# Last three third-matrix groups as split products, with the next attention and some remainders moved

## The chip, the cores and the metric

The kernel runs on one core of a Trainium2 chip. The metric is the device time of one execution in microseconds. Three runs of the kernel before took 1400.58 to 1402.51 us, median 1401.87 us. A separate profiled execution took 1403.44 us; the span of the kernel's own instructions in it is 1401.6 us.

## The reference

Attention without softmax, then two feed-forward stages, all in float32. Eight batches of eight heads, 576 tokens, 64 values per head:

```
kv  = einsum('bhsd,bhse->bhde', k, v)
out = einsum('bhsd,bhde->bhse', q, kv)
out = out / sqrt(mean(out*out, -1) + 1e-6) * g_norm
x   = out as (4608 tokens, 512)
g   = softplus(x @ w_in)                     # 512 -> 2048
x   = g @ w_out                              # 2048 -> 512
h   = max(x @ w1, x @ w2, x @ w3)            # 512 -> 768, three matrices
y   = h @ moe2_w_out                         # 768 -> 512
```

The weights arrive as float64 words and are made into float32 on the chip.

## The kernel before, in words

The tokens are done in five passes (`run_pass`), each of two halves of 456 or 464 tokens. A pass runs four layers in turn: the first (H groups, `w_in`), the second (X groups, `w_out`), the third (nine groups 16 to 24, three matrices for each of three row blocks, ended by an elementwise maximum) and the output layer. Every 2x2 block product is done in seven products instead of eight (numbered 1 to 7), so right sides and weights need sums and differences first (`combine`, `combine32`, `sums_of_weights`).

A product comes in two forms. In the first pass it is float32: two matmul calls of one column block each, which the profile shows as two instructions each, so four per product; the left side is the float32 sum of weights `sw`. In the later passes it is split: each operand is a float32r part `hi` and a float32r remainder `lo`, and a product has three float32r matmuls per block (`mm3`, lines 137 to 139), six in all. The split weights are kept as units: `make_unit` (line 302) casts a pair of sums on ScalarE (line 121) and subtracts on GpSimd (line 127), and `keep_first` stores the unit to memory for the later passes. For groups from `LATE` on, the sums themselves are stored (`keep_sums`) and the second pass splits them (`split_ahead`, `keep_ahead`).

The weights of the first pass go through these steps: SP loads raw words (line 239); ScalarE makes two parts of them (lines 250 and 252); VectorE joins them into `sw` (lines 257 and 261); GpSimd makes the four other sums (lines 130 and 133); then products read them and units are made. There are three buffers of `sw`, three of raw words, four of units `u` and two of single units `u3`.

The attention of the next pass runs beside the third layer of this one (`attention_beside`, line 654): kv products of a batch (line 471), `kv_evict` with two casts and two subtractions, and for each of eight pairs of a half and a head pair a q load, `split_q`, six matmuls `out_mm`, `square`, two matmuls `ssq_mm` and `norm`.

The order is written out by hand. Each step is put down with `at(t, ...)`, where t counts slots of one product each; the nine groups of the third layer begin at `base2`, seven slots apart, and `base2` is slot 119 of the first pass. Steps are issued in the order of t. A scheduler then orders each engine's instructions by readiness, except where an engine is pinned to the written order: all engines up to slot 1, SP for most of the kernel, and SP and ScalarE from two slots before the third layer of the first pass to its end. Slots are an order and no times: an engine goes on when its inputs are there.

Of the kernel before, what the change touches and what calls it, by code (L numbers as in the profile page):

```python
# [8 lines left out]
F32 = mybir.dt.float32  # L9
F32R = mybir.dt.float32r  # L10
# [25 lines left out]
SLOT = {1: 0, 5: 1, 6: 3, 2: 4, 7: 6, 4: 9, 3: 12}  # L36
ORDER = (1, 5, 6, 2, 7, 4, 3)
U_BUFS, U3_BUFS, GE_BUFS = 4, 2, 14
LATE = 23
FIRST_SLOT = {1: -72.2, 2: -71.5, 5: -71, 6: -69.3, 7: -67, 4: -66.4, 3: -66}  # L40
FIRST_DONE = {2: -67.9}
SECOND_SLOT = {**SLOT, 1: -75, 2: -73.7}
# [7 lines left out]
def kernel(  # L50
# [181 lines left out]
        return [w123[2 * f + i, j] for i in range(2)]  # L232

    raws, jobs = {}, []
    BESIDE = {(2, 0), *((g, 1) for g in range(1, 15) if g != 2)}

    def load_raw(key, src):
        raw = pools["raw"].tile([P, DM, 2], I32, tag="raw", bufs=3, name="raw")
# [53 lines left out]
    def sums_of_weights(g, halves=(0, 1)):  # L292
        w = sw[g]
        a11, s1, s2, a12, s3, a22, s4 = (w[:, place(g)[m]] for m in (1, 5, 6, 2, 7, 4, 3))
        if 0 in halves:
            sub(nc.gpsimd, s3, a11, s1)
            add(nc.gpsimd, s1, s1, a22)
        if 1 in halves:
            sub(nc.gpsimd, s2, s1, a11)
            sub(nc.gpsimd, s4, a12, s2)  # L300

    def make_unit(g, k):
        ms = UNITS[k]
        u = unit_tile(len(ms), 0)
        j = PLACE[ms[0]]
        src = sw[g][:, j:j + len(ms)]
        hi, lo = u[:, :, 0:256], u[:, :, 256:512]
        split(nc.scalar, src, hi, lo, nc.gpsimd)
        units[0, (g, k)] = u

    def keep_first(key):
# [52 lines left out]
    def product(p, g, m, rhs, banks):  # L364
        tag = BANK[m]
        first = m in (1, 5, 2)
        if first:
            banks[tag] = psum(tag, f"{tag}{'hxo'[(g >= 8) + (g >= 16)]}")
        acc = banks[tag][:, 0:NS[p]]
        if p == 0:  # L370
            w = sw[g][:, PLACE[m]]
            for c in range(2):
                nc.tensor.matmul(acc, w[:, c * P:(c + 1) * P], rhs[m, c], start=first and c == 0,  # L373
                                 stop=c == 1, skip_group_check=not first)
            return
        k, i = UNIT_OF[m]
        u = units[p, (g, k)]
        for c in range(2):
            xh, xl = rhs[m, c]
            wh, wl = u[:, i, c * P:(c + 1) * P], u[:, i, 256 + c * P:256 + (c + 1) * P]  # L380
            mm3(acc, wh, wl, xh, xl, first and c == 0, c == 1, not first)
# [272 lines left out]
    def attention_beside(pas, t0):  # L654

        n = NS[pas]

        for t, tt, dts in ((0, t0 - 9, (0, 2, 6, 9)), (1, t0 + 16, (0, 3, 6, 9))):
            for b in new_batches(pas, t):

                for p in range(NP):
                    at(tt + (dts[p] - 10 if p < 2 else dts[p - 2] + 0.15), load_kv, b, p)
                    at(tt + dts[p] + 0.1, kv_mm, b, p)
                at(tt + dts[3] + (0.2 if t == 0 else 1.35), kv_evict, b)
        for k in range(2 * NP):
            h, p = divmod(k, NP)
            a = TOK[pas] + h * n
            t = t0 + 8 + 6 * k
            at(t - (12 if pas == 1 else 6), load_q, a, n, p)
            at(t - 3, split_q, a, n, p)  # L670
            at(t + 0.3, out_mm, a, n, p)
            at(t + 0.4, square, a, n, p)
            at(t + 4.8, ssq_mm, a, n, p)
            at(t + 4.9, norm, a, n, p)

    def run_pass(pas, base):
# [5 lines left out]
        def weights_at(t, g, slot=SLOT):  # L682
            if pas == 0:
                for i in range(2 if g > 2 else 0):
                    jobs.append((t - 9 + 3 * i, (g, i), raw_of(g)[i], convert, (g, i)))
                if g > 2:
                    at(t - 5.9, sums_of_weights, g)
                if g >= LATE:
                    at(t + 1, keep_sums, g)
                for k in range(4 if g < LATE else 0):  # L690
                    tk = t + 1.6 * k + (4 if g > 15 else 0)
                    at(tk if g else (-69.1, -57, -56.5, -56)[k], make_unit, g, k)
                    at(tk + (2.5 if g > 15 else 5) if g else (3, 9, 9.5, 10)[k], keep_first, (g, k))
            else:
                for k, ms in enumerate(UNITS):

                    own = k == 0 and g != 17
                    lead = (8 if g == 0 else 5.9) if own else LEAD
                    at(t + min(slot[m] for m in ms) - lead, load_unit, pas, (g, k), len(ms), own)
# [89 lines left out]
        def combine_max(fp, steps):  # L789
# [5 lines left out]
            else:  # L795
                tile = ctile if steps in ((0,), (2,)) else partial(ge_tile, pas)
                combine(tile, R3, fp, tiles, steps, None, (1, 2, 7, 4, 3))

        for k in range(9):
            fp, j = divmod(k, 3)  # L800
            t = base2 + 7 * k
            slot = {**SLOT, 3: 9.9} if k == 8 else SLOT
            if pas and k < 2:
                slot = {**SLOT, 1: -6, 2: -1.8} if k == 0 else {**SLOT, 1: -10}
            weights_at(t, G_2[fp][j], slot)
            run_group(t, pas, G_2[fp][j], R2,
                      sums(lambda w, src, fp=fp, j=j: h2_done(fp, j, w, src),
                           lambda w, j=j: ((ge_tile(pas, f"m{w}", N), True) if j == 0
                                          else (ctile(f"m{w}", N), w == 22))), slot)
# [137 lines left out]
    at(T[7] + 0.75, sums_of_weights, 0, (0,))  # L947
    at(T[7] + 0.8, first_x, 1, 5)
    at(T[8] + 0.85, first_x, 0, 6)
    at(T[8] + 0.855, sums_of_weights, 0, (1,))  # L950
    at(T[8] + 0.86, first_x, 0, 7)
    at(T[9] + 0.25, first_x, 1, 6)
    at(T[9] + 0.86, first_x, 1, 7)
# [39 lines left out]
    for t, _, fn, args in events:  # L993
# [2 lines left out]
            pools["ge"] = ctx.enter_context(tc.tile_pool(name="gep", bufs=1, reuse_waits="tile"))  # L996
        if t < PIN:
            pinned(fn, args)
        elif third - 2 <= t < bases[1] - 1:
            pinned(fn, args, (mybir.EngineType.SP, mybir.EngineType.Activation))  # L1000
        elif t < GATE or fn in (kv_mm, load_kv) and t < bases[1]:
            with after([i for e, i in last.items() if e is not mybir.EngineType.SP]):
# [69 lines left out]
```

## Time and profile before

| what | us |
|---|---|
| median of three runs | 1401.87 |
| the profiled execution | 1403.44 |
| its span | 1401.6 |
| TensorE busy | 1382.8 |
| VectorE busy | 815.9 |
| ScalarE busy | 747.4 |
| GpSimd busy | 722.5 |

PE is TensorE, DVE is VectorE, ACT is ScalarE, POOL is GpSimd, SP issues most DMAs. The profile is of one execution; times in it count from the start of the span. The first pass takes about the first 350 us, its third layer about 213 to 326 us. A name such as Xo<-t,sw says what an instruction writes and reads: X, Y and W are the result banks, and the letter behind is h, x, o or y for the four layers. In the rows, "[0.57 <-DVE og L571]" is idle time of the engine just before the instruction, and what ended it.

### The profile page before, as it was taken

How to read it: one execution, taken by the hardware profiler on the slowest of the kernel's cores; microseconds unless marked ns; L12 is line 12 of the kernel's file. 1: busy time of each engine (PE TensorE's matmuls, PEld its weight loads, DVE VectorE, ACT ScalarE, POOL GpSimd, SP SyncE). 2: the span in 40 equal slices, each digit the busy share in tenths (PEclk: the TensorE clock that was granted, in tenths of full speed). 3: DMA queues.
4: the chain of work that ended last, by engine and by line, in shares of the span. 5: the costliest groups of instructions: out<-in, count | busy, mean ns of one | idle time of the engine just before them, and what ended most of it. 6: DMA issues, size and time to landing. Idle time of an engine off the chain costs nothing.

```text
span 1401.6 us, 18519 instructions
## 1 busy us (share of the span) xinstructions
PE 1382.8 (99%) x6086; PEld 1108.9 (79%) x6086; DVE 815.9 (58%) x1291; ACT 747.4 (53%) x1427; POOL 722.5 (52%) x658
## 2 busy tenths in 40 slices
PE   8999999999999999999999999999999999999998
PEld 6444455554788889888888898888888888999897
DVE  5655566886455656754457477455556764457544
ACT  6776626784465446636443565464446645443332
POOL 3899776777364444444345343353464434335320
PEclk9999999999999999999999999999999999999999
DMA  7588687886799867576667875866676667666675
GB/s 279 203 299 285 249 299 280 291 277 196 263 331 332 306 230 263 193 261 217 205 211 227 264 236 165 283 208 207 209 233 207 196 229 237 213 211 209 210 210 179
DMA packets 122143, 336.51 MB, mean 240 GB/s; under 512 B 13120, under 2 KB 33472, under 8 KB 122048
## 3 DMA queue, kind: packets, MB, share of 16 engines
q1 hardware_dynamic: 121472, 334.35, 72.2%
q8 instruction: 49, 0.80, 0.2%
q10 hardware_dynamic: 576, 0.98, 0.2%
q14 instruction: 46, 0.38, 0.1%
HBM read 269.88 MB, written 65.40 MB: 239 GB/s over the span
## 4 chain that ended last, share of the span: by engine, by line
PE 89%; DMA 4%; POOL 3%; DVE 2%; ACT 1%; issue 1%; SPq 0%; POOLq 0%; DVEq 0%
PE Xo L137 4%; PE Xo L373 4%; PE Xo L138 4%; PE Xo L139 4%; PE Xx L137 4%; PE Xx L139 4%; PE Xx L138 4%; PE Xh L137 4%; PE Xh L138 4%; PE Xh L139 4%; PE Xx L373 3%; PE Xh L373 2%; PE Yo L373 2%; PE Yo L139 2%; PE Yo L138 2%; PE Yo L137 2%
## 5 line engine op out<-in xcount | busy, mean ns | idle before, releaser
L127 POOL TENSOR_TENSOR lo<-e,hi 128x464 fp32r<-128x464 f32 (+1 forms) x160 | 188.1, 1208 | 183.9 <-ACT hi L121 172.4
L121 ACT COPY m<-Xo 128x464 f32<-128x464 f32 (+1 forms) x135 | 72.8, 545 | 107.2 <-PE Xo L139 75.0
L121 ACT CAST hi<-t 128x464 fp32r<-128x464 f32 (+1 forms) x120 | 65.7, 548 | 116.9 <-DVE e L133 48.0
L127 POOL TENSOR_TENSOR u<-sw,u 128x512 fp32r<-128x512 f32 x92 | 109.9, 1216 | 20.0 <-ACT u L121 20.0
L130 DVE TENSOR_TENSOR x<-x,Xx 128x464 f32<-128x464 f32 (+1 forms) x120 | 75.5, 632 | 57.7 <-PE Xx L139 52.2
L133 POOL TENSOR_TENSOR e<-e 128x464 f32<-128x464 f32 (+1 forms) x40 | 47.4, 1186 | 104.2 <-DVE t L133 103.7
L127 DVE TENSOR_TENSOR lo<-t,hi 128x464 fp32r<-128x464 f32 (+1 forms) x120 | 76.0, 637 | 35.2 <-ACT hi L121 33.1
L121 ACT CAST hi<-e 128x464 fp32r<-128x464 f32 (+1 forms) x160 | 85.5, 583 | 20.1 <-PE Yx L138 16.8
L137 PE MATMUL Xo<-hi,u 128*128 128x464 f32 (+1 forms) x224 | 84.6, 380 | 1.1 <-ACT m L121 0.6
L130 DVE TENSOR_TENSOR Wh<-h,Wh 128x464 f32<-128x464 f32 (+1 forms) x40 | 25.7, 642 | 98.9 <-PE Wh L139 72.9
L138 PE MATMUL Xo<-lo,u 128*128 128x464 f32 (+1 forms) x224 | 83.1, 371 | 0.0
L139 PE MATMUL Xo<-hi,u 128*128 128x464 f32 (+1 forms) x224 | 83.0, 371 | 0.0
L157 ACT ACTIVATE e<-h 128x464 f32<-128x464 f32 (+1 forms) x80 | 47.3, 592 | 65.5 <-DVE h L130 65.0
L133 POOL TENSOR_TENSOR sw<-sw 128x256 f32<-128x256 f32 x84 | 67.3, 801 | 20.7 <-DVE sw L261 11.0
L127 POOL TENSOR_TENSOR lo<-m,hi 128x464 fp32r<-128x464 f32 (+1 forms) x40 | 47.8, 1213 | 58.3 <-ACT hi L121 58.3
L121 ACT COPY h<-Xh 128x464 f32<-128x464 f32 (+1 forms) x108 | 58.5, 544 | 31.7 <-PE Xh L139 28.3
L614 POOL TENSOR_TENSOR og<-og,r 128x464 f32<-128x464 f32 (+1 forms) x32 | 41.5, 1298 | 62.0 <-DVE r L610 62.0
L138 PE MATMUL Xh<-lo,u 128*128 128x464 f32 (+1 forms) x194 | 72.5, 374 | 0.0
L137 PE MATMUL Xh<-hi,u 128*128 128x464 f32 (+1 forms) x194 | 72.2, 372 | 0.0
L139 PE MATMUL Xh<-hi,u 128*128 128x464 f32 (+1 forms) x194 | 72.0, 371 | 0.0
L137 PE MATMUL Xx<-hi,u 128*128 128x464 f32 (+1 forms) x192 | 71.4, 372 | 0.0
L139 PE MATMUL Xx<-hi,u 128*128 128x464 f32 (+1 forms) x192 | 71.3, 371 | 0.0
(269 smaller groups left out, 4122.3 us busy)
## 6 DMA issues: line engine op xcount, KB each, us to landing
u<-wd SPq DMA_DIRECT2D x241, 512.0 KB, 4.5
ux<-wd SPq DMA_DIRECT2D x99, 512.0 KB, 3.6
wd<-u SPq DMA_DIRECT2D x69, 512.0 KB, 5.4
u<-wd SPq DMA_DIRECT2D x104, 256.0 KB, 4.0
raw<-in_w_out_dram SPq DMA_DIRECT2D x22, 512.0 KB, 4.5
k<-in_kp_dram SPq DMA_DIRECT2D x31, 320.0 KB, 5.2
v<-in_vp_dram SPq DMA_DIRECT2D x29, 320.0 KB, 5.7
raw<-in_w_dram SPq DMA_DIRECT2D x18, 512.0 KB, 4.6
```

Of the source, the lines that this page charges most:

```text
L121: nc.scalar.copy(hi, src)
L127: eng_lo.tensor_tensor(out=lo, in0=src, in1=hi.bitcast(F32), op=ALU.subtract)
L130: eng.tensor_tensor(out=o, in0=a, in1=b, op=ALU.add)
L133: eng.tensor_tensor(out=o, in0=a, in1=b, op=ALU.subtract)
L137: nc.tensor.matmul(acc, wh, xh, start=first, stop=False, skip_group_check=on)
L138: nc.tensor.matmul(acc, wh, xl, start=False, stop=False, skip_group_check=on)
L139: nc.tensor.matmul(acc, wl, xh, start=False, stop=last, skip_group_check=on)
L157: tables["used"].append(nc.scalar.activation(out, src, func, **kw).ins)
L373: nc.tensor.matmul(acc, w[:, c * P:(c + 1) * P], rhs[m, c], start=first and c == 0, stop=c == 1, skip_group_check=not first)
L614: nc.gpsimd.tensor_tensor(out=og, in0=og, in1=r, op=ALU.mult)
```

## The change

It has these parts:

1. `FAST = 22`: in the first pass, groups 22, 23 and 24 (the last matrix row block of the third layer) take split products of six float32r matmuls instead of float32 ones. Their right sides are split by the new `split_third`: 14 casts on ScalarE, and 14 remainders in turn on VectorE and GpSimd; eight of them stand early in the third layer, six shortly before their use.
2. `LATE` goes from 23 to 25: groups 23 and 24 get units in the first pass, stored like the others, and the second pass splits only the output layer's weights ahead. `FAST_LEAD` places the units of groups 22 to 24 some 3.2 to 4 slots before their product; those of group 21 lose their delay of four slots.
3. The attention of the second pass is moved: the first pair 22 slots sooner, with seven slots from pair to pair instead of six; the kv products of its two halves 15 and 18.5 slots sooner. ScalarE and SP are pinned to the written order from 28 slots before the third layer instead of two.
4. In all later passes the first q load of a pass stands four slots earlier.
5. The third unit (products 7 and 4) of groups 2 to 11 has its remainder on VectorE instead of GpSimd.
6. One conversion (14, 1) uses another result bank.
7. At the start, the sums of group 0 are made in another order on GpSimd: one of them before the difference of the state that stood ahead of it.

```diff
@@ -36,7 +36,8 @@
 SLOT = {1: 0, 5: 1, 6: 3, 2: 4, 7: 6, 4: 9, 3: 12}
 ORDER = (1, 5, 6, 2, 7, 4, 3)
 U_BUFS, U3_BUFS, GE_BUFS = 4, 2, 14
-LATE = 23
+LATE = 25
+FAST, FAST_LEAD = 22, (3.4, 3.2, 3.2, 4)
 FIRST_SLOT = {1: -72.2, 2: -71.5, 5: -71, 6: -69.3, 7: -67, 4: -66.4, 3: -66}
 FIRST_DONE = {2: -67.9}
 SECOND_SLOT = {**SLOT, 1: -75, 2: -73.7}
@@ -232,7 +233,7 @@
         return [w123[2 * f + i, j] for i in range(2)]
 
     raws, jobs = {}, []
-    BESIDE = {(2, 0), *((g, 1) for g in range(1, 15) if g != 2)}
+    BESIDE = {(2, 0), *((g, 1) for g in range(1, 14) if g != 2)}
 
     def load_raw(key, src):
         raw = pools["raw"].tile([P, DM, 2], I32, tag="raw", bufs=3, name="raw")
@@ -295,8 +296,9 @@
         if 0 in halves:
             sub(nc.gpsimd, s3, a11, s1)
             add(nc.gpsimd, s1, s1, a22)
-        if 1 in halves:
+        if 1 in halves or 2 in halves:
             sub(nc.gpsimd, s2, s1, a11)
+        if 1 in halves or 3 in halves:
             sub(nc.gpsimd, s4, a12, s2)
 
     def make_unit(g, k):
@@ -305,7 +307,7 @@
         j = PLACE[ms[0]]
         src = sw[g][:, j:j + len(ms)]
         hi, lo = u[:, :, 0:256], u[:, :, 256:512]
-        split(nc.scalar, src, hi, lo, nc.gpsimd)
+        split(nc.scalar, src, hi, lo, nc.vector if k == 2 and 1 < g < 12 else nc.gpsimd)
         units[0, (g, k)] = u
 
     def keep_first(key):
@@ -367,7 +369,7 @@
         if first:
             banks[tag] = psum(tag, f"{tag}{'hxo'[(g >= 8) + (g >= 16)]}")
         acc = banks[tag][:, 0:NS[p]]
-        if p == 0:
+        if p == 0 and g < FAST:
             w = sw[g][:, PLACE[m]]
             for c in range(2):
                 nc.tensor.matmul(acc, w[:, c * P:(c + 1) * P], rhs[m, c], start=first and c == 0,
@@ -655,7 +657,8 @@
 
         n = NS[pas]
 
-        for t, tt, dts in ((0, t0 - 9, (0, 2, 6, 9)), (1, t0 + 16, (0, 3, 6, 9))):
+        early = pas == 1
+        for t, tt, dts in ((0, t0 - (24 if early else 9), (0, 2, 6, 9)), (1, t0 + (-2.5 if early else 16), (0, 3, 6, 9))):
             for b in new_batches(pas, t):
 
                 for p in range(NP):
@@ -665,8 +668,8 @@
         for k in range(2 * NP):
             h, p = divmod(k, NP)
             a = TOK[pas] + h * n
-            t = t0 + 8 + 6 * k
-            at(t - (12 if pas == 1 else 6), load_q, a, n, p)
+            t = t0 + (-14 + 7 * k if early else 8 + 6 * k)
+            at(t - (12 if pas == 1 else 6 if k else 10), load_q, a, n, p)
             at(t - 3, split_q, a, n, p)
             at(t + 0.3, out_mm, a, n, p)
             at(t + 0.4, square, a, n, p)
@@ -688,7 +691,9 @@
                 if g >= LATE:
                     at(t + 1, keep_sums, g)
                 for k in range(4 if g < LATE else 0):
-                    tk = t + 1.6 * k + (4 if g > 15 else 0)
+                    tk = t + 1.6 * k + (4 if 15 < g < FAST - 1 else 0)
+                    if g >= FAST:
+                        tk = t + slot[UNITS[k][0]] - FAST_LEAD[k]
                     at(tk if g else (-69.1, -57, -56.5, -56)[k], make_unit, g, k)
                     at(tk + (2.5 if g > 15 else 5) if g else (3, 9, 9.5, 10)[k], keep_first, (g, k))
             else:
@@ -796,6 +801,24 @@
                 tile = ctile if steps in ((0,), (2,)) else partial(ge_tile, pas)
                 combine(tile, R3, fp, tiles, steps, None, (1, 2, 7, 4, 3))
 
+        fast = {}
+
+        def split_third(m, c, i):
+            n = NS[0]
+            hi = xc_tile("hi", n, F32R)
+            if i < 4:
+                lo = ap_.tile([P, NC, P], F32, tag="kv", bufs=4, name="lo").rearrange("p c d -> p (c d)")
+                lo = lo[:, 0:n].bitcast(F32R)
+            else:
+                lo = (gc_tile if i < 8 else xc_tile)("lo", n, F32R)
+            split(nc.scalar, R2[m, c], hi, lo, nc.gpsimd if i % 2 else nc.vector)
+            fast[m, c] = (hi, lo)
+
+        if pas == 0:
+            for i in range(14):
+                m, c = divmod(i, 2)
+                m = ORDER[m]
+                at(base2 + (9 + 2.6 * i if i < 8 else 7 * 6 + SLOT[m] - 7 + 3.2 + c), split_third, m, c, i)
         for k in range(9):
             fp, j = divmod(k, 3)
             t = base2 + 7 * k
@@ -803,7 +826,7 @@
             if pas and k < 2:
                 slot = {**SLOT, 1: -6, 2: -1.8} if k == 0 else {**SLOT, 1: -10}
             weights_at(t, G_2[fp][j], slot)
-            run_group(t, pas, G_2[fp][j], R2,
+            run_group(t, pas, G_2[fp][j], fast if pas == 0 and G_2[fp][j] >= FAST else R2,
                       sums(lambda w, src, fp=fp, j=j: h2_done(fp, j, w, src),
                            lambda w, j=j: ((ge_tile(pas, f"m{w}", N), True) if j == 0
                                           else (ctile(f"m{w}", N), w == 22))), slot)
@@ -947,7 +970,8 @@
     at(T[7] + 0.75, sums_of_weights, 0, (0,))
     at(T[7] + 0.8, first_x, 1, 5)
     at(T[8] + 0.85, first_x, 0, 6)
-    at(T[8] + 0.855, sums_of_weights, 0, (1,))
+    at(T[8] + 0.845, sums_of_weights, 0, (2,))
+    at(T[8] + 0.855, sums_of_weights, 0, (3,))
     at(T[8] + 0.86, first_x, 0, 7)
     at(T[9] + 0.25, first_x, 1, 6)
     at(T[9] + 0.86, first_x, 1, 7)
@@ -996,7 +1020,7 @@
             pools["ge"] = ctx.enter_context(tc.tile_pool(name="gep", bufs=1, reuse_waits="tile"))
         if t < PIN:
             pinned(fn, args)
-        elif third - 2 <= t < bases[1] - 1:
+        elif third - 28 <= t < bases[1] - 1:
             pinned(fn, args, (mybir.EngineType.SP, mybir.EngineType.Activation))
         elif t < GATE or fn in (kv_mm, load_kv) and t < bases[1]:
             with after([i for e, i in last.items() if e is not mybir.EngineType.SP]):
```

## Rows read from the trace of the kernel before

**Rows 1.** Of the page, busy time of each engine, share of the span, instructions.

```profile
PE 1382.8 (99%) x6086; PEld 1108.9 (79%) x6086; DVE 815.9 (58%) x1291; ACT 747.4 (53%) x1427; POOL 722.5 (52%) x658
```

**Rows 2.** TensorE's waits in the whole run: total us, times, longest.

```profile
PE Xh L373 <- ACT h L121: 2.0, 3, 0.8
...
PE o L138 <- POOL ql L127: 1.2, 1, 1.2
PE Xx L373 <- ACT x L748: 0.8, 1, 0.8
```

**Rows 3.** Timeline at the start: start us, us, engine, line, operation.

```profile
34.92 1.16 POOL L133 TENSOR_TENSOR t<-og,t 128x456 f32<-128x456 f32 x1 [0.57 <-DVE og L571]
...
36.03 2.28 POOL L133 TENSOR_TENSOR sw<-sw 128x256 f32<-128x256 f32 x2
...
37.28 1.80 PE L373 MATMUL Xh<-t,sw 128*128 128x456 f32 x4 [1.80 <-POOL sw L133]
```

**Rows 4.** TensorE's timeline in the third layer of the first pass.

```profile
300.13 1.69 PE L373 MATMUL Yo<-t,sw 128*128 128x456 f32 x4
...
302.41 3.28 PE L373 MATMUL Xo<-t,sw 128*128 128x456 f32 x8
...
305.53 1.69 PE L373 MATMUL Wo<-x,sw 128*128 128x456 f32 x4
...
307.06 1.69 PE L373 MATMUL Yo<-x,sw 128*128 128x456 f32 x4
```

**Rows 5.** TensorE's timeline in the last pass.

```profile
1309.52 0.37 PE L137 MATMUL Yo<-hi,ux 128*128 128x456 f32 x1
...
1311.99 0.37 PE L137 MATMUL Xo<-hi,u 128*128 128x456 f32 x1
```

**Rows 6.** Stretches: PE, PEld, DVE, ACT, POOL busy; clock, DMA share.

```profile
60.00:100.00 40.00, 37.14 (x95) 17.16 (x94) 21.46 (x32) 28.25 (x58) 39.21 (x43) 1.00 0.83 290
300.00:320.00 20.00, 20.00 (x58) 10.50 (x57) 15.54 (x23) 13.47 (x25) 14.29 (x15) 1.00 0.92 305
```

**Rows 7.** VectorE's waits from 50 to 140 us.

```profile
DVE sw L261 <- POOL u L127: 7.6, 2, 4.3
```

**Rows 8.** GpSimd's groups, 209 to 321 us: count | busy, mean ns.

```profile
L127 POOL TENSOR_TENSOR u<-sw,u 128x512 fp32r<-128x512 f32 x21 | 28.7, 1379 | 5.8 <-ACT u L121 5.8
L133 POOL TENSOR_TENSOR sw<-sw 128x256 f32<-128x256 f32 x27 | 23.1, 857 | 6.8 <-DVE sw L261 5.4
...
L130 POOL TENSOR_TENSOR sw<-sw 128x256 f32<-128x256 f32 x9 | 6.6, 730 | 0.6
L127 POOL TENSOR_TENSOR u<-sw,u 128x256 fp32r<-128x256 f32 x7 | 5.9, 847 | 1.8 <-ACT u L121 1.8
L133 POOL TENSOR_TENSOR m<-m,m 128x456 f32<-128x456 f32 x2 | 3.2, 1613 | 3.1 <-DVE t L133 3.1
L133 POOL TENSOR_TENSOR t<-m,t 128x456 f32<-128x456 f32 x2 | 2.7, 1362 | 0.0
```

**Rows 9.** Of the page, GpSimd's costliest group.

```profile
L127 POOL TENSOR_TENSOR lo<-e,hi 128x464 fp32r<-128x464 f32 (+1 forms) x160 | 188.1, 1208 | 183.9 <-ACT hi L121 172.4
```

**Rows 10.** Timeline in the last group of the third layer.

```profile
312.06 1.69 PE L373 MATMUL Yo<-t,sw 128*128 128x456 f32 x4
...
316.17 0.73 POOL L133 TENSOR_TENSOR sw<-sw 128x256 f32<-128x256 f32 x1 [0.45 <-DVE sw L261]
```

**Rows 11.** Timeline at the start of the third layer.

```profile
214.75 0.54 ACT L121 COPY m<-Xo 128x456 f32<-128x456 f32 x1 [13.45 <-PE Xo L373]
...
215.87 0.75 ACT L121 CAST kvh<-kvps 64x256 fp32r<-64x256 f32 x2 [0.57 <-PE kvps L471]
...
216.65 0.86 DVE L133 TENSOR_TENSOR kvl<-kvps,kvh 64x256 fp32r<-64x256 f32 x2 [1.46 <-ACT kvh L121]
```

**Rows 12.** ScalarE's waits from 98 to 209 us.

```profile
ACT u L121 <- DMA wd<-u: 12.7, 17, 2.1
```

**Rows 13.** Timeline of the second pass at its first q tile.

```profile
505.59 0.58 ACT L121 CAST qh<-qraw 128x464 fp32r<-128x464 f32 x1 [0.88 <-DMA qraw<-in_qt_dram]
```

## The prediction

> **What bounds the kernel now.** I read the page first: TensorE is busy 99% of the span, no other engine above 58% [rows 1]. So time goes only if TensorE gets less work or waits less. Its waits come next: about 13 us in the whole run, and the reader is to see whose they are. Those that the change can touch are few: 2.0 us in three waits and 0.8 us in one for ScalarE, 1.2 us for the remainder of a q tile [rows 2], and 1.8 us at the start for a sum of weights from GpSimd [rows 3]. Then TensorE's timeline, for what one product costs in either form [rows 4, 5], and the busy time by stretch, for which engine has room: GpSimd has 39.2 of 40 us taken between 60 and 100 us, and 14.3 of 20 us at the end of the third layer [rows 6].
>
> **TensorE's work.** Four float32 matmul instructions of 456 columns, one product, take from 305.53 to 307.06 us, 1.53 us [rows 4]. Twelve split matmuls of 456 columns start in 2.47 us, 0.206 us each [rows 5]; a split product has six, 1.24 us. The three groups have 21 products, so 21 x (1.53 - 1.24) = 6.1 us less. Changing form is not free: the four instructions that start at 300.13 would end at 301.66, and the six attention matmuls behind them (3 x 464 columns, 0.63 us at the rate of rows 5) let the next float32 one start at 302.41, 0.12 us late; the eight that start there need 3.12 us instead of 3.06 [rows 4]. The new groups are entered and left about three times (the last two products of the group before lie among them): 0.5 us more. The moved attention has the same matmuls as before.
>
> **Early groups.** In the first layers VectorE waits 7.6 us in two waits for GpSimd's remainders of units, because they free the buffer of the weight sums [rows 7]; its sums of the hidden state are queued behind, ScalarE's activations behind those, and TensorE then waits for ScalarE's copy of a bank [rows 2]. The change takes ten subtractions off GpSimd there, each about 1.38 us by the mean of such a row [rows 8], 13.8 us of work where it is full. On VectorE they cost about 0.7 us each, an estimate from its slower way with wider tiles on GpSimd (half of 1.38; 1.38 is the upper end), where it has 21.5 of 40 us taken [rows 6]: hidden, unless the cast ahead is late, when VectorE's sums queue behind it. Of the 2.8 us (2.0 + 0.8) I count 2.2 as gone; bounds 2.8 gained and 1.0 lost (one such wait more).
>
> Beside this stands a rule that speaks against the move: the Trainium skill's "GPSIMD Engine Reference", section "Key points", says that GpSimd shares its SBUF interfaces with VectorE and contends with its instructions that have two SBUF inputs, which these are. The trace agrees in kind: sums that have a mean of 0.73 us on one line have 0.857 us on the next [rows 8]. By the rule the relief of 13.8 us would be less by up to the 7 us that VectorE's subtractions last; the 6.8 us left are still more than the waits, so the sum by the rule would be the same.
>
> **Start.** GpSimd waits 0.57 us for og, subtracts it until 36.08 us and only then makes the sum that TensorE waits for until 37.28 us [rows 3]. With the sum first it runs from 34.35 us, when the wait begins, for half of the pair's 2.28 us, and the difference, which the same product needs, ends at about 36.6 us: 0.5 us earlier, or 0.9 with the sum at 0.73 us [rows 8]. I take 0.7 us (0 to 1.8).
>
> **Third layer: what the split groups newly wait for.** A float32 product needs only sums of weights; a split one also needs a unit (a ScalarE cast, a GpSimd remainder) and a split right side. Moving the attention frees ScalarE and VectorE of it in the last three groups, but GpSimd did only one of its operations there per head pair. From the first product of the first split group to the first of the third, TensorE has 12 split and 2 float32 products: 12 x 1.24 + 2 x 1.53 = 17.9 us. In the same order GpSimd must finish the sums of two groups (8 x 0.857 = 6.9 us), five whole units (5 x 1.38 = 6.9), one half unit (0.85), the difference pair of the maximum (1.61 + 1.36 = 3.0) [rows 8] and three odd splits (3 x 1.21 = 3.6 [rows 9]): 21.2 us, 3.3 us too much. Before, sums came 4.1 us after the start of the product behind whose bank copy their conversion is queued (312.06, 316.17) [rows 10]; GpSimd has about 2.8 us of units to fill that and the slot before, so up to 2.5 us idle come on top: 5.8 us. If the splits and the maximum fall behind the units instead, 14.6 us fit and the wait is 0. I take 3.5 us, nearest to the row sum. TensorE's products are in order, so each late unit moves all behind it. The eight early splits (one cast each, 0.58 us as in rows 13, and four remainders on each of the other two engines) lie beside groups 17 to 19, whose products need none of them: nothing, as long as sums of weights keep their lead; without it, one sum late, 0.86 us.
>
> **Attention earlier.** It enters stretches where ScalarE idles (13.45 us once, until 214.75 [rows 11]). But the first kv eviction now has one float32 product (1.53 us) between its last matmul and the product that reads it. It takes from 215.87 to 217.51 us, 1.64 us with two casts and two subtractions [rows 11]: some tenths short when both engines are free. ScalarE's order is written out there, and in that stretch its unit casts wait 12.7 us in 17 waits, at most 2.1, for stores that free their buffers [rows 12]. I take 0.5 us (0 to 2.5). The earlier k, v and q loads pass unit stores and raw loads in SP's queue; a raw load's conversion stands at least six products, some 9 us, ahead of its use: nothing, and what a late store costs is in the bound of 2.5.
>
> **Later passes.** The first q tile of a pass is loaded four slots sooner. In the second pass its cast waits 0.88 us for the load [rows 13], the remainder comes behind another subtraction, and TensorE waits 1.2 us [rows 2]: I take 0.8 gained; bounds 1.2 gained, and 1.0 lost if the earlier load holds SP's weight loads up. The eight splits ahead that leave the second pass took no time of TensorE: 0.
>
> **Sum.** -6.1 + 0.5 - 2.2 - 0.7 + 3.5 + 0.5 - 0.8 = -5.3 us. The profiled execution took 1403.44 us, its span 1401.6 and 1.84 around it; so 1398.1 for such an execution. It lies 1.57 us above the median of the runs, 1401.87, so the prediction is 1396.5.
>
> **Rivals.**
> GpSimd keeps up in the split groups, since splits and the maximum slip behind: the same sum without 3.5 us, 1393.0. For it: 5.7 of 20 us free there [rows 6]. Against: six units, two half ones and three splits put 8.3 + 1.7 + 3.6 = 13.6 us into that room.
> No net gain: GpSimd holds the split groups fully (5.8 instead of 3.5) and the early waits only change their owner (0 instead of 2.2): -0.8, 1401.0. For it: the row sum is already over the room, and early, ScalarE's casts wait for stores as well. Against: the long early waits of VectorE name GpSimd alone.
> Slower: the attention's operations stand in ScalarE's written order behind unit casts that wait for stores. Four of them (the two evictions and two squares, which TensorE needs within a few products) each behind the longest wait of 2.1 us [rows 12] are 8.4 us, against 0.5 in my sum: +2.6, 1404.4; it decides from 5.8 us of such waits on. For it: the loads of k and v fall into that stretch too. Against: ScalarE idles there.
> That the split form saves nothing is excluded by rows 4 and 5, which have the same width on the same engine.
>
> **How the numbers follow.** My forecast 0.48, GpSimd keeping up 0.20, no net gain 0.20, slower 0.12. The likeliest's own range is 1394 to 1399.5. The range of 8 in 10 reaches to the rivals on both sides: below to 1391 (the first with nearly all old waits gone as well), above to 1402.5, leaving out most of the slower case. About 0.2%, 2.8 us, is what a measurement of this kernel can tell from no change: the bounds are 1399.1 and 1404.7. Faster: 0.44 of my forecast, 0.20, and 0.03 of no net gain, 0.67. Same: 0.04, 0.16 and 0.03 of the slower case, 0.23. Slower: the rest, 0.10.
>
> **What would show it.** TensorE's busy time falls by about 6 us and split products of the last three groups start 0.206 us apart. Its waits for ScalarE's copies between 60 and 90 us and for the weight sum at 37 us shrink, and new ones on GpSimd's u appear in the last third of the third layer, 2 to 6 us. VectorE's long waits for GpSimd's u are gone. The maximum's differences and odd splits stand ahead of units on GpSimd, or else the first rival holds. A wait of the first attention product for kvh or kvl over 1 us, or unit casts waiting longer than 2.1 us for stores, would speak for the slower case. The forecast is wrong if the split groups show no wait on GpSimd, or waits over 6 us.

## The result

The changed kernel took 1417.16 us (median of four runs, 1416.96 to 1417.94), the kernel before 1401.22 us beside it: a ratio of 1.011, 95% interval 1.0097 to 1.0122. It is some 16 us slower, where 5 us less were forecast.

TensorE's busy time on the page stays as in [rows 1], where about 6 us less were forecast: what the split form saves is spent again, for the larger part at a low clock, as shown below.

```profile
PE 1383.0 (98%) x6128; PEld 1117.7 (79%) x6128; DVE 827.1 (58%) x1304; ACT 751.8 (53%) x1441; POOL 726.1 (51%) x659
```

Where the time went, by the starts of TensorE's products: the first layer of the first pass ends 1.3 us earlier than before (170.8 for 172.1 us); the third layer begins 5.8 us later (218.8 for 213.0), a part of it moved attention work; it lasts 121.7 us from its first to its last product for 112.6; the pass ends 14.7 us later (373.1 for 358.4). The later passes keep about that distance, 14.5 us at the end of the span. TensorE's waits in the changed kernel, to be read beside [rows 2]:

```profile
PE Xo L138 <- ACT u L122: 7.0, 3, 5.7
PE Xo L140 <- POOL u L128: 3.5, 3, 2.0
PE Xx L375 <- DVE x L131: 2.6, 2, 1.7
...
PE Xh L375 <- ACT h L122: 1.6, 3, 1.0
PE o L139 <- DVE ql L128: 1.5, 1, 1.5
PE o L139 <- POOL ql L128: 1.2, 1, 1.2
...
PE Xh L375 <- POOL t L134: 1.0, 1, 1.0
```

10.5 us are new waits for units u, all in the third layer. The longest, 5.7 us, is read backwards in the timeline around it (start us, us, engine, line, operation; SPq is SP's DMA queue):

```profile
290.65 0.93 ACT L122 CAST u<-sw 128x512 fp32r<-128x512 f32 x2 [0.39 <-DMA wd<-u]
291.02 0.69 DVE L262 SCALAR_TENSOR_TENSOR sw<-raw,cv 128x512 int32<-128x512 int32 x1
291.78 0.33 SPq L240 DMA_DIRECT2D raw<-in_w_dram  x1
292.20 4.63 SPq L188 DMA_DIRECT2D wd<-u  x5
...
297.65 0.62 ACT L122 CAST u<-sw 128x512 fp32r<-128x512 f32 x1 [5.65 <-DMA wd<-u]
...
299.58 0.75 PE L138 MATMUL Xo<-hi,u 128*128 128x456 f32 x1 [5.72 <-ACT u L122]
...
302.24 0.58 PE L140 MATMUL Xo<-hi,u 128*128 128x456 f32 x1
302.62 0.58 PE L138 MATMUL Yo<-hi,u 128*128 128x456 f32 x1
```

The product waits for a cast, the cast for a store to free a unit buffer, and five stores stand in SP's queue behind a raw load that waited for the join at 291.02 to end. A store takes 5.7 us from issue to landing (median of the page, 5.4 before). After the idle time split matmuls start 0.38 us apart instead of 0.206 [rows 5]: the granted clock fell to its lower level, 1.2 GHz (0.50 of 2.4), as the stretches show (busy us of PE, PEld, DVE, ACT, POOL; then the clock). Before, and in the kernel without split groups, it was 1.00 there.

```profile
299.00:305.00 6.00, 5.19 (x13) 4.06 (x14) 1.96 (x4) 5.94 (x11) 3.17 (x4) 0.50 0.37 150
316.00:319.00 3.00, 3.00 (x10) 2.63 (x9) 1.04 (x2) 1.77 (x4) 3.00 (x3) 0.50 0.49 109
```

### The profile page after: what moved, and what is told of

It is laid out like the page before. It is cut to its first block, busy times and chain, and to the rows that moved or that the text cites. A ratio compares the mean times of both kernels' runs of the same rounds, so it can differ in the third digit from the quotient of the medians.

```text
span 1416.1 us, 18618 instructions
## 1 busy us (share of the span) xinstructions
PE 1383.0 (98%) x6128; PEld 1117.7 (79%) x6128; DVE 827.1 (58%) x1304; ACT 751.8 (53%) x1441; POOL 726.1 (51%) x659
## 4 chain that ended last, share of the span: by engine, by line
PE 70%; DMA 3%; ACT 2%; POOL 2%; DVE 2%; issue 1%; SPq 0%; POOLq 0%; DVEq 0%; ACTq 0%
PE Xo L138 4%; PE Xo L140 4%; PE Xo L139 4%; PE Xx L138 3%; PE Xx L139 3%; PE Xh L138 3%; PE Xx L140 3%; PE Xh L139 3%; PE Xh L140 3%; PE Yo L139 2%; PE Yo L140 2%; PE Yo L138 2%; PE Yh L138 2%; PE Yh L140 2%; PE Yh L139 2%; PE Yx L140 2%
## 5 line engine op out<-in xcount | busy, mean ns | idle before, releaser
L122 ACT CAST hi<-t 128x464 fp32r<-128x464 f32 (+1 forms) x126 | 69.1, 548 | 118.7 <-DVE e L134 53.8
L128 POOL TENSOR_TENSOR u<-sw,u 128x512 fp32r<-128x512 f32 (+1 forms) x90 | 107.8, 1212 | 34.5 <-ACT u L122 32.3
L138 PE MATMUL Xo<-hi,u 128*128 128x464 f32 (+1 forms) x248 | 95.4, 387 | 8.1 <-ACT u L122 7.0
L128 DVE TENSOR_TENSOR lo<-t,hi 128x464 fp32r<-128x464 f32 (+1 forms) x123 | 79.5, 649 | 37.4 <-ACT hi L122 35.0
L140 PE MATMUL Xo<-hi,u 128*128 128x464 f32 (+1 forms) x248 | 93.2, 376 | 3.5 <-POOL u L128 3.5
L139 PE MATMUL Xo<-lo,u 128*128 128x464 f32 (+1 forms) x248 | 92.7, 374 | 0.0
L122 ACT CAST u<-sw 128x512 fp32r<-128x512 f32 (+1 forms) x100 | 55.5, 563 | 46.8 <-DMA wd<-u 40.1
L134 POOL TENSOR_TENSOR sw<-sw 128x256 f32<-128x256 f32 x84 | 68.6, 817 | 18.0 <-DVE sw L262 14.5
L138 PE MATMUL Xx<-hi,u 128*128 128x464 f32 (+1 forms) x192 | 71.6, 373 | 0.0
```

The lines of the kernel that those rows point to most:

```text
L122: nc.scalar.copy(hi, src)
L128: eng_lo.tensor_tensor(out=lo, in0=src, in1=hi.bitcast(F32), op=ALU.subtract)
L134: eng.tensor_tensor(out=o, in0=a, in1=b, op=ALU.subtract)
L138: nc.tensor.matmul(acc, wh, xh, start=first, stop=False, skip_group_check=on)
L139: nc.tensor.matmul(acc, wh, xl, start=False, stop=False, skip_group_check=on)
L140: nc.tensor.matmul(acc, wl, xh, start=False, stop=last, skip_group_check=on)
```

## The experiments

Diffs are against the changed kernel unless said otherwise. "Third layer" is the time from the start of its first product to that of its last, in the first pass.

**The parts alone.** `no_split` leaves the split groups away:

```diff
-LATE = 25
-FAST, FAST_LEAD = 22, (3.4, 3.2, 3.2, 4)
+LATE = 23
+FAST, FAST_LEAD = 99, (3.4, 3.2, 3.2, 4)
...
-                    tk = t + 1.6 * k + (4 if 15 < g < FAST - 1 else 0)
+                    tk = t + 1.6 * k + (4 if g > 15 else 0)
...
-        if pas == 0:
+        if False:
             for i in range(14):
```

> The changed kernel without the split groups (groups 22 to 24 in float32, units of 23 and 24 from the second pass as before); the moved attention and the small parts stay. Stores theory (unit casts wait for stores of units that fall together, the idle halves the clock): the wait of 5.7 us and the low clock are gone, 1400 to 1404 us. GpSimd theory (too much work for it in the split groups): the same, 1400 to 1404. Moved-attention theory (its steps in the second layer cost the time): 1410 or more.

1404.04 us, ratio 1.0016 (1.0007 to 1.0026); third layer 109.5 us. So parts 1 and 2 of the change cost about 13 us.

`late_attention`:

```diff
-        early = pas == 1
+        early = False
...
-        elif third - 28 <= t < bases[1] - 1:
+        elif third - 2 <= t < bases[1] - 1:
```

> The changed kernel with the attention where it was before; split groups and small parts stay (eight remainders lie in other buffers, since the kv tiles are taken). Stores theory: units still fall together and the attention stands among them, 1410 to 1420 us. GpSimd theory: two of its operations more in the split groups, 1415 to 1422. Moved-attention theory: 1396 to 1402.

(Eight remainders' buffers and the bank of part 6 go back with it.) 1415.36 us, 1.0095 (1.008 to 1.011), third layer 130.2 us with all of the attention in it, where the kernel before has 112.6. The attention's place is not the main cause; with it late, TensorE waits 4.3 us for an attention cast as well.

`small_parts` has both edits (parts 4, 5 and 7 are left; the bank of part 6 goes back with the attention, so that the "one bank" of the second expectation is not in it), `small_again` is the same kernel with more rounds.

> The kernel before with only the small parts: ten remainders on VectorE, the order at the start, the q load four slots sooner. Every theory: 1398 to 1401 us, some 1 to 3 us less than before by shorter waits for ScalarE between 60 and 90 us and for the weight sum at 37 us.

> Again only the small parts (third remainders of the first layers on VectorE, the order of the first sums, the q load, one bank), attention in its old place and no split groups, with more rounds: 1400.5, a ratio of 0.999 to 1.000. If these parts are worth something: below 0.9985 with its whole interval.

1400.53 us, 0.9994 (0.9984 to 1.0003), and 1399.26 us, 0.9992 (0.9983 to 1.0000). Both point to about 1 us gained, which isn't told from nothing. It is the best version here, and not shown to beat the kernel before. By difference, the moved attention costs about 3 us.

**One link at a time.** `units_spread` lets the units' delay fall from 4 slots to 0 over six groups, so that no two groups' units fall together:

```diff
-                    tk = t + 1.6 * k + (4 if 15 < g < FAST - 1 else 0)
+                    tk = t + 1.6 * k + (4 - 0.8 * (g - 16) if 15 < g < FAST else 0)
```

> The changed kernel, but the delay of the units falls from four slots at group 16 to none at group 21 in steps of 0.8, instead of four for 16 to 20 and none for 21, so that units of groups 20 and 21 no longer fall together. Stores theory: the cast's wait of 5.7 us falls under 2 us, the clock stays at its upper level there, 1403 to 1409 us. GpSimd theory: its work is the same, 1413 to 1418. Moved-attention theory: 1413 to 1418.

1413.94 us, 1.0087 (1.007 to 1.0103), where the GpSimd theory had put it. The longest wait is gone, but TensorE now waits 4.8 us for u from GpSimd and 2.3 for u from ScalarE, and the clock still falls, three times for 3.4 us.

`no_stores`:

```diff
     def keep_first(key):
+        if key[0] >= 19:
+            wd[key] = wd[15, key[1]]
+            return
         keep(key, units[0, key])
```

> The changed kernel without the stores of the units of groups 19 to 24; the later passes read the units of group 15 in their place, so these products are computed from other weights. Stores theory (unit casts wait for buffers that stores hold): the 5.7 us wait and those like it go, 1403 to 1408 us. GpSimd theory (its sums and remainders come too late in the split groups whatever the buffers do): at most the first wait shrinks, 1410 to 1416.

1416.14 us, 1.0097 (1.0082 to 1.0112). No cast waits for a store in that stretch, and the same product is late all the same, by 2.5 us instead of 5.7; the time is at the upper end of what the GpSimd theory had named. The timeline shows what comes last now:

```profile
287.41 6.07 POOL L128 TENSOR_TENSOR u<-sw,u 128x512 fp32r<-128x512 f32 x5
...
290.37 0.69 DVE L262 SCALAR_TENSOR_TENSOR sw<-raw,cv 128x512 int32<-128x512 int32 x1
...
293.43 0.73 POOL L134 TENSOR_TENSOR sw<-sw 128x256 f32<-128x256 f32 x1
294.11 1.27 POOL L128 TENSOR_TENSOR u<-sw,u 128x512 fp32r<-128x512 f32 x1
295.33 0.73 POOL L131 TENSOR_TENSOR sw<-sw 128x256 f32<-128x256 f32 x1
296.10 0.92 ACT L122 CAST u<-sw 128x512 fp32r<-128x512 f32 x2 [5.78 <-POOL sw L131]
...
296.77 0.48 PE L138 MATMUL Xo<-hi,u 128*128 128x456 f32 x1 [2.54 <-ACT u L122]
```

Freed of stores, the casts come in a row, and so do their remainders: GpSimd subtracts five units of earlier groups (6.07 us) while the joined weights of group 22 wait for their sums from 291.1 to 293.4 us, and a sixth before the second sum.

`units_on_vector`:

```diff
-        split(nc.scalar, src, hi, lo, nc.vector if k == 2 and 1 < g < 12 else nc.gpsimd)
+        split(nc.scalar, src, hi, lo, nc.vector if g >= FAST or k == 2 and 1 < g < 12 else nc.gpsimd)
```

> The changed kernel with the remainders of all units of groups 22 to 24 on VectorE instead of GpSimd (12 subtractions, some 14 us of GpSimd's work). GpSimd theory: the waits for its u (3.5 us) go and sums come earlier, 1408 to 1412 us. Stores theory: the first wait of 5.7 us and the low clock behind it stay, 1411 to 1415.

1416.9 us, 1.0106 (1.0091 to 1.0121), above both ranges: waits for odd splits from GpSimd 4.1, u from ScalarE 3.4, bank copies 2.2 us.

`warm_split` keeps TensorE working where it had idled:

```diff
+        if p == 0 and m == 1:
+            for _ in range(20 if g == FAST else 10):
+                nc.tensor.matmul(acc, ones, kvs[0][0].rearrange("p a b -> p (a b)")[:, 0:NS[p]], start=True, stop=True)
         for c in range(2):
             xh, xl = rhs[m, c]
```

> The changed kernel with extra matmuls on constants ahead of the first product of each split group (20, 10 and 10 of 456 columns, 0.2 us each; their result is overwritten). They fill time in which TensorE waits. If the low clock behind these waits costs what its length says (10.2 us at half speed, some 5 us), the clock stays at its upper level and the time falls to 1411 to 1413 us; if the waits alone set the time, it stays at 1415 to 1418; if the extra matmuls push on what waits for TensorE, 1419 or more.

1415.28 us, 1.0092 (1.0077 to 1.0107). The clock is 1.00 throughout the third layer, which still takes 121.0 us, 8.3 of it the 40 added matmuls. The low clock is not why there are waits; what it adds to them is read from the starts of the matmuls (below), since the time is in the range for waits alone.

`combined` has the edits of `units_spread` and `units_on_vector`, and conversions sooner:

```diff
-                    jobs.append((t - 9 + 3 * i, (g, i), raw_of(g)[i], convert, (g, i)))
+                    jobs.append((t - 9 + (3 if g < FAST else 1) * i, (g, i), raw_of(g)[i], convert, (g, i)))
...
-                    at(t - 5.9, sums_of_weights, g)
+                    at(t - (5.9 if g < FAST else 7.9), sums_of_weights, g)
```

> The changed kernel with three edits: unit delays falling step by step to group 21, remainders of units of groups 22 to 24 on VectorE, and the second conversion and the sums of these groups two slots sooner. If stores and GpSimd's lateness are the whole cost of the split groups, 1396 to 1402 us, near the kernel with late float32 groups less 6; if the chain from bank copy to conversion, sums, cast and remainder is too long for six short slots in any case, 1405 to 1411.

1415.0 us, 1.0093 (1.0076 to 1.011). That is above both ranges; casts wait for stores again (12.2 us between 209 and 342, longest 6.2).

`one_group` has FAST = 24.

> Only group 24 takes split products, 22 and 23 stay float32; all else as in the changed kernel. If the cost lies in entering the split form (the products of group 22 came 8 to 9 us late, those of 23 and 24 another 3 to 5 us each): 1410 to 1413, with one wait for u of 4 us or more. If it is spread evenly over the groups (13 us over three): 1407 to 1409. If a single split group has its supply in time, and only a second one in a row runs short: 1401 to 1404.

1414.7 us, 1.0093 (1.0076 to 1.011). That is above every range. One group costs 10.7 us more than none, three cost 13.1; by the prediction's 0.29 us for each product one group saves 2.0 us and three 6.1, so some 13 of 19 us are paid with a single split group (the units of 22 and 23 are made in the first pass here too). TensorE waits 4.1 us for its first u from ScalarE and 2.6 us from GpSimd, and the same product of the groups 23 and 24 starts 19.7 us apart (310.68, 330.42), where 10.7 are usual in the kernel without split groups (307.92, 318.63). In the changed kernel and in this one the delay of the units ends one group ahead of FAST, so that units of three groups meet there.

**Several links at once.** `joint_relief` has the edits of `no_stores`, the sooner conversions, and no remainder of these on GpSimd; `gpsimd_free` is the same with stores:

```diff
-        split(nc.scalar, src, hi, lo, nc.vector if k == 2 and 1 < g < 12 else nc.gpsimd)
+        split(nc.scalar, src, hi, lo, nc.vector if g >= 19 or k == 2 and 1 < g < 12 else nc.gpsimd)
...
-            split(nc.scalar, R2[m, c], hi, lo, nc.gpsimd if i % 2 else nc.vector)
+            split(nc.scalar, R2[m, c], hi, lo, nc.vector)
```

> Several links relieved at once: remainders of the units of groups 19 and later and all splits of the right side on VectorE (none on GpSimd), conversions and sums of groups 22 to 24 two slots sooner, and the units of group 19 and later are not stored (later passes read those of group 15, other weights). Supply theory: GpSimd's queue and the stores together made the wait, each alone being replaced by the other; together gone, 1400 to 1405, third layer 105 to 111 us. Chain theory (the written order of ScalarE, bank copy to conversion to join to sums to cast to remainder, is longer than a split group, whatever the load of the engines): 1411 to 1416, third layer 118 us or more.

> As the joint relief, but with all stores of units as in the changed kernel. GpSimd theory (its burst of five to eight remainders of groups 20 and 21 ahead of the sums of group 22 is the cause): 1400 to 1405. Supply theory of two links: the casts wait for stores instead, 1408 to 1413. Chain theory: 1411 to 1416.

1412.42 us, 1.0076 (1.0059 to 1.0092), and 1414.88 us, 1.0092 (1.0076 to 1.0109). Both times lie in the chain theory's range; the first one's third layer, 116.6 us, lies between the two theories, nearer to the 118 of the chain theory. So the two links are not the whole cost, and the chain stays a rival up to `supply_free`. With GpSimd free and stores kept, the store is what comes last:

```profile
290.91 0.97 POOL L134 TENSOR_TENSOR sw<-sw 128x256 f32<-128x256 f32 x1 [4.80 <-PE Wo L375]
291.20 7.52 SPq L188 DMA_DIRECT2D wd<-u  x6
...
296.55 0.92 ACT L122 CAST u<-sw 128x512 fp32r<-128x512 f32 x2 [6.62 <-DMA wd<-u]
```

`stores_by_gpsimd` is `gpsimd_free` with those stores taken out of SP's queue:

```diff
-        nc.sync.dma_start(out=wd[key], in_=u.rearrange("p i n -> p (i n)").bitcast(F32))
+        eng = nc.gpsimd if 19 <= key[0] < LATE else nc.sync
+        eng.dma_start(out=wd[key], in_=u.rearrange("p i n -> p (i n)").bitcast(F32))
```

> As the kernel with GpSimd free, but the stores of the units of group 19 and later are issued by GpSimd, which has room then, instead of SP, where they stand behind raw loads that wait for a join. Nothing is left out. If their place in SP's queue is what makes the casts wait: ScalarE's waits for stores fall from 10.5 us to under 5, 1404 to 1409. If their way to memory (5 to 7 us from issue to landing) is what counts with four buffers: waits of 8 us or more stay, 1411 to 1416.

1410.47 us, 1.0066 (1.0052 to 1.0079), 1.5 us above the range. ScalarE's wait for stores between 285 and 335 us is nearly gone, so it was the place in SP's queue and hardly the way to memory (4.8 us from issue to landing there, 5.6 with GpSimd free). First with GpSimd free, then this kernel:

```profile
ACT u L122 <- DMA wd<-u: 10.5, 4, 6.6
...
ACT u L122 <- DMA wd<-u: 0.7, 1, 0.7
```

`given_units` leaves the units of the split groups away, `given_no_stores` adds the edit of `no_stores`, `supply_free` those of `joint_relief`:

```diff
         ms = UNITS[k]
+        if g >= FAST:
+            units[0, (g, k)] = units[0, (21, k)]
+            return
         u = unit_tile(len(ms), 0)
```

> This kernel leaves out the units of groups 22 to 24: no cast and no remainder of them, and their split products read the units of group 21 (other weights); raw loads, conversions, sums, the splits of the right side and all stores stay. Supply theory (the split groups wait for their weights, through conversion, sums, cast and remainder): with the last two links gone TensorE finds its units ready, the third layer takes 104 to 108 us instead of 121.7, no stretch at the half clock, 1398 to 1402. Form theory (the split groups are slow of themselves, through the right sides' splits, the bank copies behind them or the clock): the third layer stays over 114 us, 1408 or more.

1411.83 us, 1.0072 (1.0056 to 1.0089), third layer 115.0 us: both where the form theory had put them. The timeline shows another reason. No split product can wait for a unit of its own group, and still a store stops TensorE: the cast of one of group 21's units waits for it, and a bank copy stands behind the cast in ScalarE's written order.

```profile
296.76 0.93 ACT L122 CAST u<-sw 128x512 fp32r<-128x512 f32 x2 [5.21 <-DMA wd<-u]
...
301.76 0.95 ACT L122 COPY m<-Xo 128x456 f32<-128x456 f32 x2
...
302.33 3.41 PE L378 MATMUL Xo<-t,sw 128*128 128x456 f32 x4 [5.11 <-ACT m L122]
```

> The changed kernel without the units of groups 22 to 24 (their products read those of group 21) and without stores of units of group 19 and later (later passes read those of group 15); the remainders stay on GpSimd. Supply theory: ScalarE had waited 5.2 us for a store with a bank copy behind it; without the store that copy comes in time, third layer 105 to 109 us, 1399 to 1404. If GpSimd's remainders of groups 20 and 21 hold the sums of group 22: a wait of 2 to 4 us for m or for hi, and 1404 to 1409. Form theory: 1405 to 1412.

1407.0 us, 1.0041 (1.0027 to 1.0055), third layer 111.5 us: in the ranges of the second and third theory. In the third layer no wait for u or m is left; odd splits from GpSimd are waited for, 3.8 us.

> The joint relief and the given units together: units of groups 22 to 24 are not made (their products read those of group 21), units of group 19 and later are not stored (later passes read those of group 15), the remainders of units of groups 19 to 21 and all splits of the right side are on VectorE, conversions and sums of groups 22 to 24 stand two slots sooner. Supply theory: nothing is left to wait for, the third layer takes 104 to 108 us, 1398 to 1402. Form theory (changes of form, half clock, splits of the right side): third layer 112 us or more, 1405 to 1412, with few waits on u or m.

1403.69 us, 1.0018 (1.0009 to 1.0027), third layer 108.4 us, no half clock in it: just above the supply theory's ranges and well under the form theory's. So the split groups are not slow of themselves; but with the supply given away they only draw level with late float32 groups (1404.04 us). TensorE's waits from the start of the third layer on:

```profile
PE o L139 <- DVE ql L128: 1.6, 1, 1.6
PE Xo L139 <- DVE lo L128: 1.2, 1, 1.2
PE kvps L479 <- DMA v<-in_vp_dram: 0.8, 2, 0.6
PE Yo L138 <- DVE m L798: 0.3, 1, 0.3
PE Wo L138 <- DVE m L798: 0.3, 1, 0.3
```

The third layer by what was relieved, us:

| kernel | third layer | of it at the lower clock |
|---|---|---|
| changed kernel | 121.7 | 10.2 |
| no stores | 119.9 | 6.8 |
| GpSimd free, conversions sooner | 120.4 | 10.2 |
| the same, stores out of SP's queue | 116.3 | 6.8 |
| GpSimd free, conversions sooner, no stores | 116.6 | 6.8 |
| units given | 115.0 | 6.8 |
| units given, no stores | 111.5 | 3.4 |
| GpSimd free, conversions sooner, no stores, units given (`supply_free`) | 108.4 | 0 |
| without split groups | 109.5 | 0 |

Each row is one profiled execution, and part of the differences is the clock. Stores alone are worth 1.8 us there and GpSimd alone (with sooner conversions) 1.3, both together 5.1. By the ratios of the runs they are worth 1.8 and 2.5 alone and 4.8 together, which is no more than the sum within the intervals; that one link comes last when the other is relieved is seen in the timelines above. With the supply gone entirely 13.3 us come back. It is the supply of split weights as a whole that costs, cast and remainder with it; how the 13.3 us divide among its links stays open.

## Why the prediction was wrong

**TensorE's work: right, and changing form costs nothing.** Split matmuls start 0.206 us apart where nothing is late. In `supply_free` the third layer is 1.0 us shorter than without split groups: -6.1 of the prediction, and back come 1.8 for ql, 1.5 for lo and 1.1 for m, which makes -1.7; the other 0.7 us lie in several delays of 0.2 us or less. These waits are listed above with 1.6, 1.2 and 0.6 us only, since the list counts from the modelled end of the matmul before, 0.37 us after its start, where the next start is due after 0.206; and the matmul behind a wait is late as well. Behind the first wait for m, listed with 0.27 us, the starts are 0.64 and 0.31 us apart, 0.53 us more than two usual ones (first three rows):

```profile
296.63 0.37 PE L140 MATMUL Xo<-hi,u 128*128 128x456 f32 x1
297.27 0.47 PE L138 MATMUL Wo<-hi,u 128*128 128x456 f32 x1 [0.27 <-DVE m L798]
297.58 0.37 PE L139 MATMUL Wo<-lo,u 128*128 128x456 f32 x1
...
300.22 1.69 PE L381 MATMUL Xo<-t,sw 128*128 128x456 f32 x4
301.40 0.73 PE L138 MATMUL Xo<-hi,u 128*128 128x456 f32 x1
301.96 0.37 PE L139 MATMUL Xo<-lo,u 128*128 128x456 f32 x1
302.17 0.37 PE L140 MATMUL Xo<-hi,u 128*128 128x456 f32 x1
```

The 0.5 us that the prediction took for changes of form shows in no run. The float32 product at 300.22 is due to end at 301.75, by its 1.53 us, and the second split matmul is then due at 301.96, where it starts: the first one starts 0.35 us early and holds the next by as much longer. In [rows 4] the late start came from short pieces of the attention, 112 columns, which start 0.11 us apart where their width asks for 0.05:

```profile
302.19 0.27 PE L138 MATMUL o<-ql,kvh 128*128 128x112 f32 x1
302.30 0.27 PE L139 MATMUL o<-qh,kvl 128*128 128x112 f32 x1
```

**Third layer, what the split groups newly wait for: the step that failed.** I took 3.5 us with 5.8 as the upper bound; the changed kernel has 10.5 us of such waits. GpSimd's row sum was a right reading of one link only. The wait for stores was left out of this step: before, ScalarE's waits in the third layer name no store, with units delayed by four slots and no product that reads one. The change took away both: a cast that waits for a store has a split product directly behind it, and bank copies in the same written order. ScalarE's waits there are now led by

```profile
ACT u L122 <- DMA wd<-u: 11.2, 6, 5.6
```

And the step ended at the wait: the half clock that comes with it, 10.2 us of it, costs about 4.2 us (17 starts 0.173 us late each, and 1.2 us right behind the waits and in one float32 product). The sum for the third layer against no split groups, by the starts of the matmuls: -6.1, +12.1 for the waits for u (listed with 10.5), +4.2 for the clock and +1.7 for ql are 11.9; measured are 12.2.

**The early splits: "nothing" was wrong.** In the kernels with the attention sooner the q remainder on VectorE is late by 1.4 to 1.6 us at 269 us in most of those with split groups and never in the one without; in the changed kernel one early remainder (1.19 us from 267.75) and the maximum's difference (1.71 us from 268.86) stand ahead of it on VectorE. That it is the early splits that are in its way was not tried by itself.

**Early groups: wrong in size.** Of 2.2 us nothing certain came; the small parts together, 3.7 by my terms, gained about 1. VectorE's waits of [rows 7] are still there:

```profile
DVE sw L262 <- POOL u L128: 7.1, 2, 3.9
```

GpSimd's rows between 60 and 172 us say why (count | busy, mean ns | idle before). Before, 34 whole units took 44.6 us with 8.8 us idle ahead of them; now:

```profile
L128 POOL TENSOR_TENSOR u<-sw,u 128x512 fp32r<-128x512 f32 x25 | 33.5, 1340 | 16.2 <-ACT u L122 16.2
L134 POOL TENSOR_TENSOR sw<-sw 128x256 f32<-128x256 f32 x33 | 27.2, 825 | 1.3
...
L128 DVE TENSOR_TENSOR u<-sw,u 128x512 fp32r<-128x512 f32 x10 | 9.6, 955 | 2.3 <-ACT u L122 2.0 <-POOL e L134 0.3
```

Of 11.1 us saved, 7.4 became waiting for ScalarE's casts, and 1.6 went into slower sums (825 ns each; 774 before). The latter agrees in kind with the sharing of SBUF interfaces that the prediction weighed from the Trainium skill ("GPSIMD Engine Reference", "Key points"), but is small. Of the 84 subtractions of this row in the whole trace before, the 59 with no VectorE operation on two SBUF operands beside them take 0.73 us each, none over 0.75, and the 25 with one beside them 0.97 us on average; in the changed kernel 33 of 84 have one. The remainder on VectorE took 0.955 us, not 0.7.

**Start: nothing gained.** The 1.8 us for the sum [rows 3] became 1.0 and 0.5 us for two differences t and 0.4 us for a join of weights on VectorE. **Later passes: nothing gained;** the wait for ql in the second pass is still 1.2 us: the cast no longer waits for its load, but its remainder stands on GpSimd behind another subtraction as before, where an earlier load doesn't help. (The waits of TensorE before add up to 14.6 us by its list, not to about 13; nothing rests on it.)

**Attention: mis-sized.** 0.5 us was taken, 2.5 was the bound, about 3 were measured. 1.7 us of it is one product behind x; in the timeline without split groups, from which alone this is read, VectorE does the attention's r and, after a long t, a join first:

```profile
211.16 0.64 DVE L612 SCALAR_TENSOR_TENSOR r<-t,r 128x464 f32<-128x464 f32 x1
...
212.31 0.98 DVE L134 TENSOR_TENSOR t<-x,t 128x456 f32<-128x456 f32 x1
...
213.22 0.68 DVE L262 SCALAR_TENSOR_TENSOR sw<-raw,cv 128x512 int32<-128x512 int32 x1
213.81 0.62 DVE L131 TENSOR_TENSOR x<-x,Xx 128x456 f32<-128x456 f32 x1
...
214.49 1.80 PE L375 MATMUL Xx<-t,sw 128*128 128x456 f32 x4 [1.69 <-DVE x L131]
```

0.7 us more is v's load (1.0 for 0.3 us). The kv eviction that I had feared shows no wait.

**The rivals.** The slower one, at 0.12, had the right mechanism, casts behind stores in ScalarE's written order, with the wrong place (attention instead of split products) and too low a price (8.4 us against 10.5 and what the clock adds). Its sign came: casts wait longer than 2.1 us for stores, up to 5.6. The prediction's own test, waits on GpSimd over 6 us, came true in its total and misled in its owner: 3.5 us are put down to GpSimd, within the 2 to 6 us that were to be seen, and 7.0 to ScalarE, behind which stores and GpSimd stand in turn.

## What to carry to other kernels

When an operation is given a new input, follow that input's whole supply back (cast, sums, buffers, the store that frees the buffer, the queue of that store) and ask of each link how late it may be today unnoticed; the row that shows waiting without harm is the price once the consumer moves up. A link relieved alone shows little where a second is nearly as late: relieve them together, or give the input away, before a theory is dropped. And a wait of TensorE costs more than the list says: measure it by the starts of the matmuls around it, and look at the clock behind it.

## What the runs showed of the hardware

TensorE's clock fell to its lower level with waits: in the changed kernel during one of 5.7 us, and it stayed low for 6.8 us, and behind one of 2.0 us, for 3.4 us; in `joint_relief` for 6.8 us with no wait in the third layer above 1.9 us. With matmuls filled into the waits it did not fall there. Going from a float32 product to split matmuls costs nothing that the starts show (300.22 to 301.96 us above). A listed wait of 0.27 us moved the matmuls behind it by 0.53 us. Subtractions of 128x256 on GpSimd took 0.73 us alone and 0.97 us beside a VectorE operation on two SBUF operands. A unit's store needs 5.7 us to land, so with four buffers its place in the queue counts: taking it out of SP's queue removed nearly all of a 10.5 us wait.
